# Two unused 32-byte tiles that shift every tile of on-chip memory by 32 bytes

## The chip, the cores and the metric

The kernel runs on one core of one Trainium2 chip. TensorE (PE) multiplies matrices, VectorE (DVE), ScalarE (ACT) and GpSimd (POOL) work element by element, SyncE (SP) issues nearly all transfers. All share the on-chip memory: 128 partitions, and a tile takes the same byte range of each. Products go to eight banks of accumulation memory. A matmul has two operands in on-chip memory: the stationary one, which a weight load (PEld) brings into the array, and the moving one, which streams through, one column at a time. The metric is the device time of one execution in microseconds, as a median of several runs.

## The reference

```python
mod = (_silu(c) @ w_mod).reshape(c.shape[0], 6, 1, -1)
sa, ca, ga, sb, cb, gb = (mod[:, 0], mod[:, 1], mod[:, 2], mod[:, 3], mod[:, 4], mod[:, 5])
h = _layernorm(x, axis=-1) * (1 + ca) + sa
x = x + ga * _A_ref(h, A_wqkv, A_wo)
h = _layernorm(x, axis=-1) * (1 + cb) + sb
x = x + gb * _B_ref(h, B_w1, B_b1, B_w2)
```

x is 2048 rows of 448 numbers in float32. `_A_ref` is attention with 16 heads of width 28 over a sliding window of 256 rows; `_B_ref` is a dense layer from 448 to 1792, mish (x tanh(softplus(x))), and a dense layer back to 448. The modulation vectors come from c, one row.

## The kernel before

The rows are worked in four groups of 512 (g = 0 to 3). To hold float32 accuracy, each operand of a large product is split into a high part, in TensorE's rounded float32 format, and a low part, the rest; a product is then three passes per 128 of the inner size (high by high, high by low, low by high), eleven matmuls over 448 inner rows.

Three stages follow each other. In the first 40 us the first rows of x, the modulation weights and the projection weights are loaded and split, and the first q and k tiles are made (L490). From there to about 440 us attention runs, head by head: `A` makes scores for the row maxima (sA, L675, read by DVE with the mask at L677), `M2` turns the maxima and sends them into the q tile by a transfer, `B` makes the shifted scores (sB, L705, and masks through L716), ACT takes the exponential twice (L719, L720), POOL makes the low part (L727), `PV` multiplies by v (pv, L737), `E` turns the result (L751), and POOL scales it into the tile `on` (L767). Between these steps a list of fillers issues the projections of the next group (qk and qk_v, L311), the output projection (wo, L311) and the normalisations, at a rate written out by hand. From about 440 us the dense layers run in 56 steps, 14 for each group: eleven matmuls for z (L912, moving operand the normalised rows `hh` and `hl`, weights from `w13` and `w1l`), mish on ACT (L918), a split (L919, L920), and twelve matmuls for the output of the step before (acc, L1095 to L1097, moving operand `w2h` or `w2l`, weights `ah` or `al`). The program text gives the order of the instructions on every engine; the allocator doesn't change it.

On-chip memory is a pair of stacks of pools. The left stack grows upward, in this order: `cst` (constants, among them `cT`, `ident`, `ones`, `cols`), `mid` (hh, hl, output weights, `on`), `vp` (six of the ten v tiles), `kq` (k tiles, mask, first q tile), `st0` (staging for the first loads), which `att` (other q tiles, P, Ph, Pl) replaces at L510, and later `ff` in the place of vp, kq and att (L1084). The right stack grows downward from the end: `vq` (four v tiles), `qk` (x tiles, `wq3`, `wql`), and later `w1p` in the place of both (L824; it holds w13, w1l, ah, al, t) and `tmp` (L826). A tile takes a multiple of 32 bytes. By the allocator's listing of this kernel the tiles start as follows, in bytes of a partition:

| tile | stack | start | beyond a multiple of 64 |
|---|---|---|---|
| cT, ones, cols | left | 16512, 17088, 17600 | 0 |
| ident | left | 16544 | 32 |
| hh (and all of mid) | left | 19680 | 32 |
| v0 / k3_0 / P | left | 62944 / 85984 / 126752 | 32 |
| xin / wq3 / wql | right | 147488 / 155680 / 177184 | 32 |
| w13 / w1l / ah | right | 148832 / 177504 / 219104 | 32 |
| v6 | right | 213984 | 32 |

The right stack ends at 229344; the left one reaches 147232 at its highest, while the right one begins at 147488. The large tiles are all 32 beyond; rows inside them step by multiples of 64 bytes, except the heads of v (240 bytes each) and of `on` (112 bytes each).

Of the kernel before, what the change touches and what calls it, by code (L numbers as in the profile page):

```python
# [8 lines left out]
F32 = mybir.dt.float32  # L9
# [42 lines left out]
def adaln_block(ctx: ExitStack, tc: tile.TileContext, x, wqkv, wo, w1, b1, w2, c, w_mod, out):  # L52
# [8 lines left out]
    def pool(name, side="left", space=None):  # L61
        kw = {} if space is None else {"space": space}
        cm = tc.tile_pool(name=name, bufs=1, reuse_waits="tile", side=side, **kw)
        st = ExitStack()
        return st.enter_context(cm), st
# [4 lines left out]
    cst, cst_s = pool("cst")  # L70
    mid, mid_s = pool("mid")
    vp, vp_s = pool("vp")
    kq, kq_s = pool("kq")
    st0, st0_s = pool("st0")
    vq, vq_s = pool("vq", side="right")
    qk, qk_s = pool("qk", side="right")
    ctx.enter_context(tc.manual_schedule())

    cT = cst.tile([112, 4], F32, name="cT")
    nc.scalar.dma_start(cT, c.rearrange("o (k p) -> p (o k)", p=112))  # L80
    ACT.add_instruction(mybir.InstLoadActFuncSet(
# [697 lines left out]
    FW = {}  # L779
# [177 lines left out]
    def fill_side(g):  # L957
        if g + 1 < NG:
            yield from ln1[g + 1]
            while g + 1 not in ht_done:  # L960
                yield
            yield from lazy((gen_mod_wo, lambda: gen_mod_ln2(3), lambda: gen_mod_ln2(4))[g])
            if g == NG - 2:
                yield from gen_out_load()
            return
        yield from gen_out_sum()
        while g not in w1_ready:
            yield
        yield from gen_w1()
# [12 lines left out]
    side = {g: fill_side(g) for g in range(NG)}  # L982
# [43 lines left out]
    for u in range(NU + 9):  # L1026
        s, k = divmod(u, 3)
# [56 lines left out]
    ff, ff_s = pool("ff")  # L1084
# [41 lines left out]
    def fill_step():  # L1126
        if fill is not None:
            pipe.step()
            next(fill, None)
            flush()  # L1130
    for n in range(NN + 1):
# [14 lines left out]
        if n:  # L1146
# [2 lines left out]
            ff2(n - 1)  # L1149
            for _ in range(1 + (g == 0) + (n == 1)):  # L1150
                fill_step()
    for st in (ff_s, mid_s, cst_s, FW["s"], psf_s):
        st.close()


# [21 lines left out]
```

## Time and profile before

| what | us |
|---|---|
| median of three runs | 720.67 |
| the runs | 719.48, 723.41, 720.67 |
| span of the profiled execution | 719.3 |

The page of the profile gives busy time by engine, the chain of work that ended last (followed backward from the last instruction, at each step to what released it), and groups of instructions by line. Matmuls are pipelined: one starts before the one before it ends, so their busy times overlap, and what one costs is the distance of its start from the next start. The chain view shows that: its pieces follow each other without overlap. The rows themselves stand in the prediction.

### The profile page before, as it was taken

What the parts mean: (1) busy time and instruction counts of PE and PEld (TensorE: products, weight loads), DVE (VectorE), ACT (ScalarE), POOL (GpSimd) and SP (SyncE); (2) the same over time, 40 slices, a digit from 0 to 9 for tenths busy, and PEclk for the clock granted to TensorE, in tenths of its full rate; (3) what the DMA queues carried; (4) which work ended last, traced back from release to release, by engine and by line L of the source; (5) the groups of instructions that cost most, each with busy time, mean ns of one, the idle gap of its engine ahead of it and who ended that gap; (6) DMA issues with size and microseconds to landing.
All of it is one profiled execution on the core that took longest, in us unless ns stands there. A gap on an engine that the chain in (4) does not pass through costs nothing.

```text
span 719.3 us, 12057 instructions
## 1 busy us (share of the span) xinstructions
PE 694.8 (97%) x4049; PEld 595.9 (83%) x4049; DVE 380.0 (53%) x1018; ACT 390.8 (54%) x740; POOL 326.5 (45%) x358
## 2 busy tenths in 40 slices
PE   8899999999999999999999899999999999999996
PEld 8777778788898788898887688888888888888885
DVE  5588657688555878555768642334223222322112
ACT  4538778767666758666878864243224222422221
POOL 6536679576765767666879754332010000000002
PEclk9999999999999999999999999999999999999999
DMA  7865854454771562744782175300200020001001
GB/s 213 258 211 178 249 185 138 136 160 139 200 217 50 178 190 75 220 158 127 227 225 75 52 237 143 108 1 14 90 1 1 13 90 1 1 13 39 0 1 51
DMA packets 48249, 83.86 MB, mean 117 GB/s; under 512 B 6142, under 2 KB 26348, under 8 KB 48188
## 3 DMA queue, kind: packets, MB, share of 16 engines
q1 hardware_dynamic: 47724, 83.10, 38.0%
q8 instruction: 32, 0.52, 0.3%
q14 instruction: 29, 0.24, 0.1%
q10 hardware_dynamic: 464, 0.00, 0.0%
HBM read 53.45 MB, written 29.36 MB: 115 GB/s over the span
## 4 chain that ended last, share of the span: by engine, by line
PE 72%; issue 11%; DVE 8%; DMA 4%; ACT 2%; POOL 1%; SPq 1%; POOLq 0%; DVEq 0%; ACTq 0%
PE z L912 15%; PE pv L737 9%; PE qk L311 8%; PE sA L675 5%; PE acc L1096 5%; PE acc L1097 5%; PE acc L1095 5%; PE sB L705 4%; PE wo L311 4%; PE qk_v L311 4%; PE sB L716 3%; DVE junk L677 3%; PE et L751 2%; DMA q<-mr 1%; PE warm L424 1%
## 5 line engine op out<-in xcount | busy, mean ns | idle before, releaser
L727 POOL TENSOR_TENSOR Pl<-P,Ph 128x512 fp32r<-128x512 f32 (+2 forms) x192 | 234.3, 1228 | 87.1 <-ACT Ph L720 48.4
L677 DVE CUSTOM_DVE_ANT_0 junk<-sA,mask 128x384 f32<-128x384 f32 (+2 forms) x256 | 135.1, 528 | 98.7 <-PE sA L675 90.1
L719 ACT ACTIVATE P<-sB 128x512 f32<-128x512 f32 (+2 forms) x192 | 109.7, 571 | 66.7 <-PE sB L716 61.0
L920 DVE TENSOR_TENSOR al<-t,ah 128x512 fp32r<-128x512 f32 x56 | 38.7, 692 | 200.0 <-ACT ah L919 200.0
L918 ACT ACTIVATE t<-z,b1c 128x512 f32<-128x512 f32 x56 | 38.5, 687 | 189.3 <-PE z L912 178.4
L720 ACT ACTIVATE Ph<-sB 128x512 fp32r<-128x512 f32 (+2 forms) x192 | 109.4, 570 | 0.0
L675 PE MATMUL sA<-k,q 84*128 84x384 f32 (+2 forms) x256 | 101.0, 396 | 2.5 <-DVE mx L677 1.5
L912 PE MATMUL z<-hhf,w 128*128 128x512 f32 x224 | 89.6, 400 | 0.0
L912 PE MATMUL z<-hlf,w 128*128 128x512 f32 x224 | 88.8, 396 | 0.0
L1095 PE MATMUL acc<-w2h,ah 128*128 128x448 f32 x224 | 82.1, 367 | 0.0
L1096 PE MATMUL acc<-w2l,ah 128*128 128x448 f32 x224 | 82.1, 367 | 0.0
L1097 PE MATMUL acc<-w2h,al 128*128 128x448 f32 x224 | 82.0, 366 | 0.0
L737 PE MATMUL pv<-Ph,v 128*60 128x256 f32 (+2 forms) x352 | 77.1, 293 | 3.5 <-DVE o L745 2.3
L737 PE MATMUL pv<-Pl,v 128*60 128x256 f32 (+2 forms) x352 | 74.2, 285 | 2.3 <-POOL Pl L727 2.3
L705 PE MATMUL sB<-q,k 86*128 86x256 f32 (+1 forms) x352 | 74.5, 285 | 1.7 <-DMA q<-mr 1.7
L912 PE MATMUL z<-hhf,w1l 128*128 128x512 f32 x168 | 66.4, 395 | 0.0
L705 PEld LDWEIGHTS sB<-q,k 86*128 86x128 f32 x352 | 62.3, 191 | 3.2 <-DMA q<-mr 1.4
L737 PEld LDWEIGHTS pv<-Ph,v 128*60 128x60 f32 x352 | 45.7, 134 | 18.2 <-ACT o L743 3.2
L716 PE MATMUL sB<-fdmask,identr 128*128 128x128 bf16 (+1 forms) x320 | 60.4, 254 | 0.0
L675 PEld LDWEIGHTS sA<-k,q 84*128 84x128 f32 x256 | 48.9, 192 | 8.9 <-DVE mx L677 5.9
L737 PEld LDWEIGHTS pv<-Pl,v 128*60 128x60 f32 x352 | 45.4, 132 | 10.9 <-POOL Pl L727 3.9
L1104 POOL TENSOR_TENSOR yo<-yo,x 128x448 f32<-128x448 f32 (+1 forms) x4 | 4.1, 1057 | 108.6 <-DVE yo L1101 108.6
(156 smaller groups left out, 1297.4 us busy)
## 6 DMA issues: line engine op xcount, KB each, us to landing
scr<-st SPq DMA_DIRECT2D x24, 512.0 KB
k<-scr SPq DMA_DIRECT2D x48, 252.0 KB
q<-scr SPq DMA_DIRECT2D x64, 168.0 KB
scr<-st SPq DMA_DIRECT2D x32, 256.0 KB
x<-x1d SPq DMA_DIRECT2D x10, 448.0 KB
xin<-in_A_x_dram SPq DMA_DIRECT2D x8, 448.0 KB
xr<-in_A_x_dram SPq DMA_DIRECT2D x16, 224.0 KB
x1d<-xr SPq DMA_DIRECT2D x16, 224.0 KB
```

The source lines that it names most:

```text
L311: PE.matmul(p, b, a, start=(n == 0), stop=(n == 10))
L675: PE.matmul(p[:, c0:384], q[0:84, t * 128:(t + 1) * 128], k[0:84, t * 128 + c0:t * 128 + 384], start=True, stop=True)
L677: DVE.tensor_tensor_reduce(out=junk[:, c0:384], in0=p[:, c0:384], in1=mask[:, c0:384], scale=1.0, scalar=-3.0e38, op0=ALU.add, op1=ALU.max ...
L705: PE.matmul(p[:, c:c + 128 * (t1 - t0)], k[:, jj * 128:(jj + 1) * 128], q[:, t0 * 128:t1 * 128], start=(n == 0), stop=False, skip_group_ch ...
L719: ACT.activation(P[:, c0:], p[:, c0:], AF.Exp, scale=SCALE)
L720: ACT.activation(Ph[u][:, c0:], p[:, c0:], AF.Exp, scale=SCALE)
L727: eng.tensor_tensor(Pl[u][:, a:b], Pt[u][:, a:b], Ph[u][:, a:b].bitcast(F32), op=ALU.subtract)
L737: PE.matmul(pv[0:60, t0 * 128:t1 * 128], V[j % NV][:, h, :], P[u][:, c:c + 128 * (t1 - t0)], start=(P is Ph and b == 0 and n == 0), stop=F ...
L912: PE.matmul(zb[n], ps[m][1], ps[m][0], start=(m == 0), stop=(m == 10))
L1095: PE.matmul(p, ah[n][:, ts], w2h[f], start=(f == 0), stop=False)
L1096: PE.matmul(p, ah[n][:, ts], w2l[f], start=False, stop=False)
L1097: PE.matmul(p, al[n][:, ts], w2h[f], start=False, stop=(f == NF - 1))
```

## The change

One tile of 32 bytes (`lead`) is allocated as the first of the left stack's first pool, and a pool `edge` with one tile of 32 bytes is opened as the first of the right stack. Nothing writes or reads them. The pool is closed at the end of the program in its turn.

```diff
@@ -72,10 +72,13 @@
     vp, vp_s = pool("vp")
     kq, kq_s = pool("kq")
     st0, st0_s = pool("st0")
+    edge, edge_s = pool("edge", side="right")
+    edge.tile([128, 8], F32, name="edge")
     vq, vq_s = pool("vq", side="right")
     qk, qk_s = pool("qk", side="right")
     ctx.enter_context(tc.manual_schedule())
 
+    cst.tile([128, 8], F32, name="lead")
     cT = cst.tile([112, 4], F32, name="cT")
     nc.scalar.dma_start(cT, c.rearrange("o (k p) -> p (o k)", p=112))
@@ -1149,7 +1152,7 @@
-    for st in (ff_s, mid_s, cst_s, FW["s"], psf_s):
+    for st in (ff_s, mid_s, cst_s, FW["s"], edge_s, psf_s):
         st.close()
```

All other tiles of the left stack move up by 32 bytes, those of the right stack down by 32: hh to 19712, k3_0 to 86016, wq3 to 155648, w13 to 148800, all multiples of 64, while cT, ones and cols come to lie 32 beyond.

## The prediction

> **What bounds the kernel now.** I read the page first (engine shares, then the chain), then the busy times by stage, then the chain inside each stage.
>
> ```profile
> span 719.3 us, 12057 instructions
> PE 694.8 (97%) x4049; PEld 595.9 (83%) x4049; DVE 380.0 (53%) x1018; ACT 390.8 (54%) x740; POOL 326.5 (45%) x358
> ...
> PE 72%; issue 11%; DVE 8%; DMA 4%; ACT 2%; POOL 1%; SPq 1%; POOLq 0%; DVEq 0%; ACTq 0%
> ```
>
> ```profile
> 0.00:40.00 40.00, 35.90 (x205) 31.43 (x206) 24.88 (x58) 18.36 (x32) 22.80 (x57) 1.00 0.80 236
> 40.00:440.00 400.00, 386.29 (x2570) 329.03 (x2569) 272.72 (x832) 289.98 (x580) 275.91 (x265) 1.00 0.54 164
> 440.00:720.00 280.00, 272.60 (x1277) 235.48 (x1276) 82.35 (x129) 82.42 (x129) 27.77 (x36) 0.99 0.10 31
> ```
>
> The columns after the stretch's length are busy time and instructions of PE, PE's weight loads, DVE, ACT and POOL, then the granted clock, the DMA share and GB/s. TensorE is busy nearly without a break at full clock; DMA fills the first 40 us only. So a change of addresses is worth what it does to TensorE's operand reads, and the other engines matter by their shares of the chain alone.
>
> ```profile
> by line: PE pv L737 15.9%; PE qk L311 14.1%; PE sA L675 8.8%; PE sB L705 7.9%; PE qk_v L311 6.4%; PE wo L311 5.8%; PE sB L716 5.4%; DVE junk L677 4.9%; PE z L912 3.2%; issue 3.1%; PE et L751 2.7%; DMA q<-mr 2.5%; DVE tr L250 1.7%; DVE hl L2
> ```
>
> This is the chain from 40 to 440 us. Its PE entries sum to 70%, 281 of 400 us. From 440 us on PE alone sets the pace. So of the matmuls about 0.70 x 2570 + 1277 = 3080 stand on the path, and 1 ns on each of them is 3.1 us.
>
> What one of them takes is read from starts on the chain, since the busy times of pipelined matmuls overlap:
>
> ```profile
> 490.53 0.44 PE trf L246 x4
> ...
> 495.95 2.57 PE z L912 x11
> ...
> 500.94 2.57 PE z L912 x11
> ...
> 511.02 2.57 PE z L912 x11
> 516.07 2.57 PE z L912 x11
> ```
>
> ```profile
> 253.19 0.47 PE pv L737 x4
> 253.66 0.24 PE sB L705 x2
> ```
>
> Eleven matmuls of 512 columns take 2.57 us, 0.2336 us each. The twelve of 448 columns between 498.52 (495.95 + 2.57) and 500.94 take 2.42 us, 0.2017 us each. In attention four pv matmuls, 1024 columns, take 0.47 us, 0.235 us per 512; two sB matmuls, 512 columns, take 0.24 us.
>
> **The change part by part.** Two tiles that nothing writes or reads are allocated, and one pool is opened and closed: no instruction, no DMA, no semaphore, no bytes moved. What changes is addresses. By the allocator's listing of the kernel before, every tile of the left stack goes up by 32 bytes and every tile of the right stack down by 32; both stacks keep their inner order, so which tile lies where another lay stays the same, and no wait for reuse is added. Between the stacks 256 bytes are free at their tightest, 192 after; no tile of one lies over one of the other. Removed and added instructions: 0 us.
>
> So every term is a rate: does an operand that starts on a multiple of 64 cost other than one that starts 32 beyond? The trace of before has controls, since some operands already start elsewhere.
>
> ```profile
> L737 PEld LDWEIGHTS pv<-Ph,v x352: 129/133/239, 50.9 to 416.9; 128*60 128x60 f32 x176
> ...
> L737 PEld LDWEIGHTS pv<-Pl,v x352: 129/131/217, 51.2 to 417.1; 128*60 128x60 f32 x176
> ```
>
> ```profile
> L912 PEld LDWEIGHTS z<-hhf,w x224: 187/188/197, 413.7 to 706.9; 128*128 128x128 f32 x112
> ```
>
> ```profile
> L552 PEld LDWEIGHTS ga<-wm,ones x2: 186/188/189, 91.1 to 91.2; 112*128 112x128 f32 x2
> ```
>
> Weight loads (three numbers: least, median, most, in ns). Head h of v starts at 32 + 240h bytes, so the heads run through 32, 16, 0 and 48 beyond a multiple of 64, a quarter each. If a quarter were quicker, the least would stand well below the median; it stands 2 to 4 ns below. The tile ones lies on a multiple of 64 now and loads in a median of 188 ns, as w13 does from 32 beyond. I price weight loads at 0, bounds -2 to +2 ns, and they overlap the running matmul anyway.
>
> ```profile
> L767 POOL TENSOR_TENSOR on<-ol,rc x32: 554/563/572, 68.2 to 422.6; 128x224 f32<-128x224 f32 x32
> ```
>
> ```profile
> 0.72 0.20 POOL masks.py:197 MEMSET ident<- 128x128 f32 x1 [0.29 <-POOLq L1165]
> ...
> 1.24 0.20 POOL L141 MEMSET ones<- 112x128 f32 x1
> ```
>
> Writes by POOL: heads in pairs advance 224 bytes in the tile on, so half of these 32 writes begin on a multiple of 64 and half 32 beyond: 554 to 572 ns, one cluster. The memsets of ident (32 beyond) and ones (a multiple) both take 0.20 us. Price 0.
>
> ```profile
> L677 DVE CUSTOM_DVE_ANT_0 junk<-sA,mask 128x384 f32<-128x384 f32 x224 | 123.9, 553 | 81.9 <-PE sA L675 77.4
> ...
> L677 DVE CUSTOM_DVE_ANT_0 junk<-sA,mask 128x256 f32<-128x256 f32 x16 | 6.7, 417 | 3.2 <-PE sA L675 2.8
> ```
>
> DVE takes (553 - 417) / 128 = 1.06 ns per element. Its 8% of the chain is 58 us, about 105 instructions of 553 ns; at most one piece of 64 bytes (16 elements, 17 ns) saved in each is -1.8 us, the other end 0. ACT's 2% is a quarter of that. DMA's 4% is 29 us; a piece of 2048 bytes over 32 instead of 33 units of 64 is at most 3%, -0.9 us. I take 0 for all three, by the POOL rows, which are nearest.
>
> The moving operand of a matmul is what no row shows: all of them start 32 beyond now. Bound from the rows: a cost at the start must show where 512 columns are cut in two. The pv pairs cost 0.235 - 0.2336 = 1.4 ns more than one matmul, the sB pairs 0.24 - 0.2336 = 6.4 ns. A start thus costs 1.4 to 6.4 ns in all, whatever its reason, and alignment can win at most this: -4 to -20 us over 3080 matmuls. The other end is a loss of the same size as two rhythms seen in the trace, priced below. Between ends that far apart I take 0, by the weight loads, the nearest reads by the same engine. The Trainium skill (SBUF — State Buffer, Specifications) gives the memory's lines as 16 bytes; 32 beyond is already on such a line, so by that rule the sum is exactly 0, while the trace agrees for weight loads only (131 and 133 ns at offsets 0 to 48).
>
> Sum: 719.3 us span + 0 = 719.3. The runs have a median of 720.67, 1.4 us above the profiled span (their least, 719.48, is 0.2 above it); with that 1.4 the forecast is 720.
>
> **The rivals.**
>
> *A start on a full line of 64 saves part of each start.* For it: a cost of 6.4 ns per start of sB is there, and z at 512 columns is slower than twice the transposes' pace would give. Against it: the pv pairs show 1.4 ns, and weight loads show nothing. Middle of 4 and 20 us: 720.7 - 12 = 709, from 701 to 716.
>
> *The whole stream is slowed by straddling.* If each 64 bytes of the stream are fetched across two lines, the cost runs with the columns. Four transposes of 128 columns take 0.44 us; if a plain pass can go at twice that pace, an estimate from this row, 512 columns take 0.22 us. Then z gains 13.6 ns x 11 and acc 9.2 ns x 12 per step, 260 ns, 14.6 us over 56 steps; in attention 0.2375 becomes 0.22, 7.4% of 281 us = 20.8 us. Result 685. Against it: the excess may be how these passes run. The Trainium skill (TensorE: Matmul & The Clock Gate, Back-to-back issue gap) gives N/2.4 + 2.5 ns, 216 ns for 512 and 189 ns for 448 columns; by it the same sum wins about 42 us, 679. The trace stands above that page by 17 ns.
>
> *Slower: the distance between the two stacks.* Left goes up and right goes down, so a matmul whose moving operand lies left and whose weights lie right sees them 64 bytes closer. That address relations may matter is seen in the step: 495.95 to 500.94 is 4.99 us, 511.02 to 516.07 is 5.05 us with the same 2.57 us in z, so twelve acc matmuls cost 2.48 instead of 2.42 us, 5 ns each, with other w2 tiles as moving operand. If the new distance puts all such matmuls into the slow rhythm: z and acc 1277, qk and qk_v (20.5% of 400 us at 0.234 us) 350, together 1627; half of acc, 336, I count as slow already, leaving 1290 x 5 ns = 6.5 us: 727. It decides from 3.6 / 1.29 = 2.8 ns per matmul. Against it: pv reads its moving operand from the left stack and v from either stack (six of its ten tiles left, four right), and the loads of v keep one median over both; no row ties the step's two rhythms to distance.
>
> *The change does not do what it says.* If an unused tile got no room, addresses stay and the time is 720.7; this falls in with the forecast.
>
> **How the numbers follow.** What differs by less than 0.5%, 3.6 us, can't be told from no change in runs that spread from 719.5 to 723.4. Chances: no effect 0.37, part of each start 0.29, the whole stream 0.12, slower rhythm 0.22. A cheap end of the second (under 3.6 us) is too small a part to move. So faster 0.41, same 0.37, slower 0.22, and the likeliest single case is 720. Cases of both signs hold most of the chance: the forecast's own range is 717 to 724. The range from 700 to 731 holds no effect, the partial gain and the slower rhythm up to 8 ns per matmul (10.3 us), and leaves out the whole-stream case and the slower tail, some 0.17.
>
> **What would show it.** Right: z still 2.57 us for eleven, acc 2.42 or 2.48 us for twelve, pv 0.47 us for four, weight loads 188 and 131 ns, and the same number of instructions in the same order. A gain at starts: z, pv and sB shorter by the same few ns whatever their columns, so sB pairs gain twice what z gains. The whole stream: the gain goes with the columns, z near 2.42 us for eleven. The slower rhythm: every step at 5.05 us or more, wo (both operands left) unchanged while z, acc and qk lengthen. The forecast is wrong if PE's starts move at all beyond 1 ns each; it is wrong in another place if PE's starts stay and DMA landings or DVE's idle time before L677 move.

## The result and the profile after

The changed kernel takes 718.18 us as a median of nine runs (716.06 to 719.96), the kernel before 720.67 in nine runs beside it (719.09 to 723.41). The ratio is 0.9966 with a 95% interval from 0.9949 to 0.9982: a gain of 2.5 us, small but not nothing. The profiled execution is the slowest of the nine, 719.96 us with a span of 718.2, where the other eight have spans from 714.3 to 717.3. So the two profiled spans, 719.3 and 718.2, understate the gain, and stages are compared below, not spans.

The page of the kernel after, busy times, the main queue and the chain by engine:

```profile
span 718.2 us, 12057 instructions
...
PE 694.9 (97%) x4049; PEld 597.3 (83%) x4049; DVE 380.0 (53%) x1018; ACT 390.9 (54%) x740; POOL 327.0 (46%) x358
...
q1 hardware_dynamic: 47724, 83.10, 37.1%
...
PE 72%; issue 11%; DVE 8%; DMA 4%; ACT 2%; POOL 1%; SPq 1%; POOLq 0%; DVEq 0%; ACTq 0%
```

The counts are the same on every engine, and their order in the two traces is too. The stretches by stage, same columns as before:

```profile
0.00:40.00 40.00, 36.74 (x206) 32.26 (x206) 25.16 (x59) 18.34 (x32) 23.04 (x57) 0.96 0.78 236
40.00:440.00 400.00, 386.69 (x2568) 329.59 (x2567) 272.52 (x831) 289.81 (x580) 276.09 (x265) 0.99 0.53 164
440.00:720.00 280.00, 271.51 (x1279) 235.44 (x1277) 82.37 (x129) 82.79 (x129) 27.83 (x36) 0.99 0.10 31
```

The granted clock reads 0.96 and 0.99 in the first two stretches where the kernel before had 1.00 twice; that belongs to this execution, the slowest of the nine. In the dense stage both have 0.99, and there the traces can be compared. The chain of the kernel after, at the places that the prediction quoted:

```profile
495.92 2.56 PE z L915 x11
...
500.91 2.56 PE z L915 x11
...
510.88 2.57 PE z L915 x11
...
515.86 2.56 PE z L915 x11
```

The step that took 4.99 us still does (500.91 - 495.92). The step that took 5.05 us now takes 4.98 (515.86 - 510.88), with the same 2.57 us in z: the gain sits in the twelve acc matmuls of the steps that were slow. Over all 56 steps, the mean from one start to the next in the trace:

```
ns from start to start           before    after
acc, 448 columns, f = 0 to 6      205.9    201.1
acc, 448 columns, f = 7 to 13     202.9    203.4
z, 512 columns                    233.0    232.8
first acc to last acc, us         291.76   290.22
```

In this table f is the place of a step among the 14 of its group. 28 steps x 12 x (-4.8 ns) + 28 x 12 x 0.5 + 56 x 11 x (-0.2) = -1.6 us, against 291.76 - 290.22 = 1.54 us measured. Of the other operations, qk went from 233.1 to 231.3 ns, qk_v from 202.1 to 203.6, wo from 205.1 to 204.2. A second trace of the kernel before, told of below, has 233.1, 202.3 and 204.2: there qk and qk_v stay where they were, while the fall of wo is no more than two traces of one kernel differ by. The controls, from the instructions by line and tile of the kernel after:

```profile
L740 PEld LDWEIGHTS pv<-Ph,v x352: 129/133/240, 50.7 to 417.4; 128*60 128x60 f32 x176
```

```profile
L915 PEld LDWEIGHTS z<-hhf,w x224: 187/188/264, 414.1 to 705.8; 128*128 128x128 f32 x112
```

```profile
L770 POOL TENSOR_TENSOR on<-ol,rc x32: 557/564/571, 67.8 to 423.2; 128x224 f32<-128x224 f32 x32
```

```profile
L680 DVE CUSTOM_DVE_ANT_0 junk<-sA,mask 128x384 f32<-128x384 f32 x224 | 123.9, 553 | 82.6 <-PE sA L678 78.1
```

Weight loads, POOL and DVE kept their times within 1 ns (medians of 133, 188 and 564 ns, and a mean of 553 for DVE). What is left is the pace at which the moving operand streams: it changed by a few ns, in some passes and not in others.

### The profile page after: what moved, and what is told of

It is laid out like the page before. It is cut to its first block, busy times and chain, and to the rows that moved or that the text cites. A ratio compares the mean times of both kernels' runs of the same rounds, so it can differ in the third digit from the quotient of the medians.

```text
span 718.2 us, 12057 instructions
## 1 busy us (share of the span) xinstructions
PE 694.9 (97%) x4049; PEld 597.3 (83%) x4049; DVE 380.0 (53%) x1018; ACT 390.9 (54%) x740; POOL 327.0 (46%) x358
## 3 DMA queue, kind: packets, MB, share of 16 engines
q1 hardware_dynamic: 47724, 83.10, 37.1%
## 4 chain that ended last, share of the span: by engine, by line
PE 72%; issue 11%; DVE 8%; DMA 4%; ACT 2%; POOL 1%; SPq 1%; POOLq 0%; DVEq 0%; ACTq 0%
PE z L915 15%; PE pv L740 9%; PE qk L314 8%; PE sA L678 5%; PE acc L1098 5%; PE acc L1100 5%; PE acc L1099 5%; PE sB L708 5%; PE wo L314 4%; PE qk_v L314 4%; PE sB L719 3%; DVE junk L680 3%; PE et L754 2%; DMA q<-mr 1%; DMA scr<-st 1%
## 5 line engine op out<-in xcount | busy, mean ns | idle before, releaser
L740 PE MATMUL pv<-Pl,v 128*60 128x256 f32 (+2 forms) x352 | 74.4, 286 | 2.3 <-POOL Pl L730 2.3
```

The source lines that it names most:

```text
L740: PE.matmul(pv[0:60, t0 * 128:t1 * 128], V[j % NV][:, h, :], P[u][:, c:c + 128 * (t1 - t0)], start=(P is Ph and b == 0 and n == 0), stop=F ...
```

## The experiments

Two theories. **Place** (A): what counts is whether an operand starts on a multiple of 64; the expectations of the first runs take this for the transfers above all. **Distance** (B): what counts is how far the moving operand lies from the weights (its address less theirs), modulo some power of two; the change moves the left stack by +32 and the right one by -32, so for a matmul with its moving operand left and its weights right the distance grows by 64. The expectations name a third, C: any displacement changes the time by chance.

**One side at a time.** The first run keeps only the tile `lead`, the second only the tile `edge`. Each aligns one of the two stacks and changes the distance by 32.

```diff
+    cst.tile([128, 8], F32, name="lead")
```

```diff
+    edge, edge_s = pool("edge", side="right")
+    edge.tile([128, 8], F32, name="edge")
...
-    for st in (ff_s, mid_s, cst_s, FW["s"], psf_s):
+    for st in (ff_s, mid_s, cst_s, FW["s"], edge_s, psf_s):
```

> Only the left stack moves (up 32 bytes, to multiples of 64); the right one stays 32 beyond. Theory A, transfers that read or write on-chip memory are dearer from 32 beyond: the packets of 1792 bytes that leave the left stack (x1d and out) take 74 ns instead of 76 to 79 ns, those of st (right stack) stay; ratio about 0.998. Theory B, the matmuls' rhythm follows the distance between the stacks: twelve acc matmuls leave 2.42 or 2.48 us by over 0.02 us, and the ratio may fall on either side of 1. Theory C, any displacement does it by chance: ratio anywhere in 0.994 to 1.006.

> Only the right stack moves (down 32 bytes). Theory A: packets from the left stack stay at 76 to 79 ns, those stored from st get shorter; ratio about 0.998, and the two halves together give the whole change (0.9966). Theory B: the distance of the stacks changes by the same 32 bytes as with the left alone, so acc and z come out as with the left alone. Theory C: no relation to the halves.

Measured: 720.05 us, ratio 1.0001 [0.9988, 1.0014], and 719.98 us, 1.0001 [0.9985, 1.0016]. The chain of the first:

```profile
576.87 2.57 PE z L913 x11
...
581.91 2.58 PE z L913 x11
...
586.96 2.58 PE z L913 x11
```

Steps of 5.04 and 5.05 us, as before. Neither alignment alone gives a half of the gain, or any that can be measured. Theory B came true in part: the two sides come out alike, as it said, but it had also expected the twelve acc matmuls to leave their 2.42 and 2.48 us by over 0.02 us, and they stay within that (a mean of 204.4 and 204.5 ns for one, 204.4 before).

**Both sides by 64 and by 96.** Both tiles as `[128, 16]`, then as `[128, 24]` (the diff of the change with this number). With 64 every large tile stays 32 beyond a multiple of 64; with 96 every one is aligned, as in the change. The distance grows by 128 and 192.

> Both tiles are 64 bytes: every tile moves by 64, so all large ones stay 32 beyond a multiple of 64. Theory A: nothing gained, ratio 1.000 within 0.0015, packets of x1d and out at 76 to 79 ns. Theory B: the distance changes by 128 bytes, twice that of the change, so the acc times change too. Theory C: a ratio other than 1 is as likely as with the change.

> Both tiles are 96 bytes: every large tile lies on a multiple of 64 again, at other places than with the change (64 beyond a multiple of 256 on the left instead of 0). Theory A with 64 bytes as the unit: ratio 0.9966 within 0.0015 as with the change, packets at 74 ns. If 256 bytes are the unit, packets stay at 76 to 79 ns and the ratio at 1.000. Theory B: the distance changes by 192 bytes, acc times other than with the change. Theory C: no relation.

Measured: 718.33 us, 0.9977 [0.9963, 0.9991], and 717.87 us, 0.9965 [0.9952, 0.9977]. The first gains without any alignment. The second has the ratio that Theory A had expected, so taken alone it would fit both theories. The chain of the first shows where the gain lies:

```profile
581.56 2.53 PE z L915 x11
...
586.54 2.53 PE z L915 x11
```

Here z takes 2.53 us for eleven and acc 4.98 - 2.53 = 2.45, 0.04 and 0.03 us less than in the steps of 5.05 us. Over all steps acc keeps its mean of 204.4 ns (1.9 ns less where f is 0 to 6, 1.9 more where it is 7 to 13), and z falls from 233.0 to 230.0: on balance the gain is in another operation than in the change.

**The pace by itself.** A kernel of matmul blocks alone, 40 each, on two tiles whose bases are a multiple of 256 bytes apart; weights step by 512 bytes. The block's first letter is its width (L 512, K 448, S 128 columns), the second the start of the moving operand (a, b, c, d, e at 0, 16, 32, 48, 96 bytes), the third that of the weights (a, c at 0 and 32); `dist` blocks move the moving operand by 0, 64, 128, 256 to 2048 bytes. Behind them stand element-wise passes and transfers at several offsets. The kernel before ran once more with it.

```python
for i in range(40):
    PE.matmul(p[i % 2][:, 0:cols], W[:, w + 128 * (i % 4):w + 128 * (i % 4) + 128], X[:, m:m + cols], start=True, stop=True)
```

> Computes nothing of the reference: loads, matmuls, element-wise instructions and stores of one shape each, with operands at 0, 16, 32, 48 and 96 bytes beyond a multiple of 256 (transfers at more places). Prediction's own step: matmul starts, weight loads, ACT, DVE and POOL equal within 1 ns at all places. Rival, a start on a line of 64 saves: 1 to 6 ns less per matmul at 0 than at 32, the same for 128 and 512 columns. Rival, the stream straddles: about 14 ns less at 0 for 512 columns, 3 to 4 ns for 128. Theory A: stores of 1792 bytes 2 to 5 ns a packet shorter from 0 and 64 than from 32 and 96; loads equal.

> The kernel before, unchanged, for the spread of a profile: PE starts and packet times of late stores (76 to 79 ns) come back as in the first profile, and the DMA queue's share within 0.3 of 38.0%. If the late stores come out at 74 ns here, Theory A falls.

The kernel before again took 718.94 us in a single run, with 204.0 and 233.0 ns for acc and z (first trace 204.4 and 233.0) and a dense stage of 291.31 us (291.76): between two traces of one kernel the dense stage moves by about 0.5 us. The chain of the blocks (start, us for 40):

```profile
53.78 9.07 PE mmLaa L74 x40
62.86 9.33 PE mmLac L74 x40
72.19 9.27 PE mmLba L74 x40
81.46 9.46 PE mmLbc L74 x40
90.92 9.33 PE mmLca L74 x40
100.25 9.07 PE mmLcc L74 x40
...
118.65 9.27 PE mmLdc L74 x40
```

For 512 columns this settles it. Both operands at 0 (aa) and both at 32 (cc) take the same 9.07 us; one of them at 32 (ac, ca) takes 9.33. A moving operand 16 bytes further than the weights takes 9.27 with the weights at 0 (ba) and at 32 (dc). The distance sets the pace, the place does not. The prediction's own step, which this run's expectation gave as equal within 1 ns, fails here: the blocks of 512 columns spread over 9.07 to 9.46 us, 226.8 to 236.5 ns each. The passes of 128 columns took 4.42 to 4.47 us for 40 at every distance. Element-wise passes don't mind either, from the view of the tile Z, each group over four combinations of offsets 0 and 32:

```profile
L89 ACT ACTIVATE Z<-Y x16: 629/629/630, 331.4 to 341.3; 128x512 fp32r<-128x512 f32 x16
...
L94 DVE TENSOR_TENSOR Z<-Y x16: 691/692/694, 342.4 to 353.3; 128x512 fp32r<-128x512 f32 x16
...
L98 POOL TENSOR_TENSOR Z<-Z,Y x16: 1262/1262/1262, 354.1 to 374.2; 128x512 fp32r<-128x512 f32 x16
```

**The same distance without alignment, and a whole period.** First `lead` alone as `[128, 16]`: the distance of the change (+64), every large tile 32 beyond. Then both tiles as `[128, 32]`: +256. Beside them the map of the pace, blocks as above with the moving operand 0 to 512 bytes further, and a version with distances chosen from the blocks above, told of below.

> Only the left stack moves, by 64 bytes: all large tiles stay 32 beyond a multiple of 64, but moving operand and weights come 64 bytes closer, as with the change. Theory B (the distance between the two operands within 256 bytes sets the pace): start to start, acc 202.3 and z 232.8 ns as with the change, dense stage 290.2 us instead of 291.8, ratio 0.9965 to 0.9985. Theory A (alignment to 64): acc 204.4, z 233.0 ns, ratio 1.000 within 0.0015.

> Both tiles are 128 bytes, distance changed by 256. Theory B with a period of 256 bytes: acc 204.4 and z 233.0 ns as before, dense stage 291.8 us, ratio 1.000 within 0.0015. If the period is longer, they differ. Theory C (any displacement): a ratio of 0.997 is as likely as in the other displacements.

> Computes nothing of the reference: matmuls of 512 and of 448 columns with the weights fixed and the moving operand 0, 32, 64 and so on up to 256, 288, 320 and 512 bytes further. Theory B: 226.7 ns at 0 and about 229 at 64 for 512 columns, 231 to 234 at 32, 96 and 128; 206.7 at 0 and 200.0 at 64 for 448 columns; 288 and 320 like 32 and 64. Theory A: equal at 0, 64, 128, 192 and another value at 32, 96, 160, 224.

With +64 by one side alone: 718.71 us, 0.9978 [0.9967, 0.9988], acc 202.3 and z 232.8 ns, which are the means of the change (202.3, 232.8), and a dense stage of 290.21 us (290.22). Its chain has steps of 4.96 and 4.99 us where the kernel before has 5.05:

```profile
576.28 2.56 PE z L913 x11
581.24 2.57 PE z L913 x11
586.23 2.56 PE z L913 x11
```

With +256: 720.31 us, 1.0006 [0.9992, 1.002], acc 204.4, z 233.0 and 291.76 us, which are those of the kernel before, and steps of 5.05 us:

```profile
578.89 2.57 PE z L915 x11
583.94 2.57 PE z L915 x11
```

So the period divides 256 bytes, and all of the dense stage's gain is distance. Theory C falls too: two pairs of kernels at other addresses but equal distances have the same dense stage within 0.01 us. The map (start, us for 40; a, b, c, d, e, f, g, h are 0 to 224 bytes in steps of 32, i 256, k 320):

```profile
53.86 9.07 PE mLa L74 x40
62.93 9.34 PE mLb L74 x40
72.27 9.16 PE mLc L74 x40
...
90.76 9.33 PE mLe L74 x40
...
109.46 9.33 PE mLg L74 x40
...
128.12 9.09 PE mLi L74 x40
...
146.55 9.16 PE mLk L74 x40
...
164.80 8.11 PE mKa L74 x40
...
181.17 8.00 PE mKc L74 x40
...
197.38 8.15 PE mKe L74 x40
...
230.06 8.27 PE mKi L74 x40
...
246.50 8.00 PE mKk L74 x40
```

For 512 columns distance 0 is the quickest (226.8 ns each), 64 next (229.0), the rest near 233. For 448 columns 64 is the quickest (200.0). At distance 0 and 256 they have two rhythms, 8.11 and 8.27 us (202.8 and 206.8 ns), though 206.7 was expected at 0. The first kernel of blocks differs in the same way between distances that are whole periods apart, 8.31 us at 0 (distp) and 8.11 at 512 (distt):

```profile
272.65 8.31 PE distp L74 x40
...
305.22 8.11 PE distt L74 x40
```

So for 448 columns the distance is not all that counts; nor is 288 quite like 32 there (8.18 and 8.27 us).

**Chosen distances.** The blocks ask for distance 0 in z and 64 in acc. In the kernel before z is at 128 and acc at 0, but for the `w2l` of f = 7 to 13, which lie 64 further. `edge` of 64 bytes brings acc to 64, a gap of 64 behind `w1l` brings z to 0, and a gap of 192 ahead of the tiles of f = 7 brings them into line. The first version leaves the left stack where it was, all large tiles 32 beyond; the second is the change with the two gaps, all aligned; the third is the first again, beside the second.

```diff
+    edge.tile([128, 16], F32, name="edge")
...
         w1l = FW["w1l"] = p1.tile([128, 3, F], F32R, name="w1l")
+        p1.tile([128, 16], F32, name="gap")
...
         pl = FW["p1"] if f == 0 else FW["ff"]
+        if f == 7:
+            pl.tile([128, 48], F32, name="gap7")
```

> Distances chosen apart for the two products: the right stack 64 bytes down, 64 unused bytes between w1l and ah, 192 in ff ahead of w2l7, so that hh and hl start at the same place within 256 bytes as w13 and w1l (0, where the rates run has 226.7 ns for 512 columns), w2h and w2l 64 beyond ah and al (200.0 ns for 448), and qk at 0. All large tiles stay 32 beyond a multiple of 64. Theory B: z 227 to 230 ns, acc 200 to 202 ns, dense stage 284 to 288 us, ratio 0.988 to 0.995. Theory A: 1.000 within 0.0015.

> The change as it is (32 bytes at each end, large tiles on multiples of 64) plus the two gaps of the run with chosen distances: the same distances (0 for z, 64 for acc, 0 for qk), but aligned. Theory B alone: z 227.8, acc 200.3 ns, dense stage 285.9 us as without alignment, and the same ratio, 0.992 within 0.0015. If alignment adds something of its own (Theory A in the transfers of the first 440 us), up to 1 us less, ratio 0.9905.

> The run with chosen distances and all large tiles 32 beyond a multiple of 64, once more on the same chip as its aligned twin, for a direct comparison: ratio 0.992 within 0.0015, z 227.8 and acc 200.3 ns.

Measured: 714.55 us, 0.9922 [0.9905, 0.9939]; 714.30 us, 0.9919 [0.9903, 0.9935]; 714.64 us, 0.9925 [0.9908, 0.9941]. All three beat both kernels. The stretch and the chain of the first:

```profile
440.00:720.00 280.00, 264.34 (x1265) 232.67 (x1263) 80.30 (x125) 80.94 (x125) 26.00 (x35) 0.99 0.10 31
```

```profile
577.56 2.49 PE z L917 x11
...
582.46 2.49 PE z L917 x11
...
587.35 2.49 PE z L917 x11
```

Steps of 4.90 and 4.89 us (acc 2.41 and 2.40), at the same granted clock of 0.99. The second, aligned, has the same 2.49 us in z and a step of 4.89:

```profile
580.31 2.49 PE z L918 x11
...
585.20 2.49 PE z L918 x11
```

With the distances equal, alignment is worth nothing that these runs can tell. All runs together, from the traces and the timings:

```
                 distance   large tiles  acc    z      dense   ratio
                 z    acc   beyond 64    ns     ns     us
before           128  0     32           204.4  233.0  291.76  1
left 32          160  32    0 / 32       204.4  233.6  291.99  1.0001
right 32         160  32    32 / 0       204.5  233.6  292.11  1.0001
the change       192  64    0            202.3  232.8  290.22  0.9966
left 64          192  64    32           202.3  232.8  290.21  0.9978
both 64          0    128   32           204.4  230.0  289.89  0.9977
both 96          64   192   0            202.9  230.8  289.38  0.9965
both 128         128  0     32           204.4  233.0  291.76  1.0006
chosen           0    64    32           200.3  227.8  285.85  0.9922
chosen, aligned  0    64    0            200.3  227.6  285.83  0.9919
```

In every row the `w2l` of f = 7 to 13 lie 64 further than the column says, but for the last two; and the w2 tiles of f = 0, which lie in the right stack with ah, are at 0 throughout. Some things the map does not give: at distance 0, z is 230.0 ns with acc at 128 and 227.8 with acc at 64 (226.8 alone), and at 64 it is 230.8 (229.0 alone). In attention qk (hh against wq3, by the listing of the tiles) went from 192 to 0 with the change and gained 1.8 ns, where the map has 6.5; qk_v, whose weights lie left and whose moving operand lies right, went from 64 to 0 and lost 1.5, where the map has 2.8 or 6.8. The signs are the map's, the sizes are not. A pass seems to depend on the pass beside it too; that was not tried by itself.

## Why the prediction was right, and where not

**The time.** 718.18 lies in both ranges that the prediction gives and 1.8 us under its forecast of 720; the ratio's interval lies within 0.5% for all but its lower end (0.9949). So the forecast of no effect within 0.5% came near, but of the zeros in its sum one was wrong. That the zero cost so little was luck: the change happens to move z between two distances of equal pace and helps one half of the acc steps only. Other shifts by unused bytes, the chosen distances, took 5.9 us off the dense stage alone, and 714.55 us lies outside 717 to 724.

**Right.** No instruction, transfer or semaphore was added, and no order changed. Weight loads, POOL, DVE and ACT cost nothing, as their rows said. z stayed at 2.57 us for eleven, and pv and sB at their durations, from the chain after:

```profile
251.56 0.47 PE pv L740 x4
252.03 0.24 PE sB L708 x2
```

The Trainium skill (SBUF — State Buffer, Specifications) gives lines of 16 bytes, from which the prediction took that 32 beyond is as good as a multiple of 64; for the place of an operand the runs agree, since 0 and 32 gave the same 9.07 us.

**The step that failed.** The prediction priced the moving operand at 0 "by the weight loads, the nearest reads by the same engine", and called itself wrong if PE's starts moved "at all beyond 1 ns each". They did: acc by 2.1 ns in the mean, by 4.8 ns where f is 0 to 6, and qk by 1.8 ns. A weight load read alone can't show this, because the price belongs to the pair, as ac and ca against aa and cc show: where the moving operand lies relative to the weights. That the stream and the weight loads beside it are what meets is argued, not shown. Nor did the bounds for the moving operand rest on much: its 6.4 ns for a start came from a row of 0.24 us, and the last digit of that row is worth 10 ns.

**The rivals.** Those of a full line and of straddling fell: aligning one side gives 1.0001 twice, the shift by 64 gains at 32 beyond, and the aligned and unaligned versions with equal distances have 0.9919 and 0.9925. The rival of the distance between the two stacks named the true mechanism, in the right place (the acc matmuls of the steps at 5.05 us) and of the right size (it said 5 ns each), but with the wrong sign: it took the kernel before to be partly in the slow rhythm and the change to put all of it there. In fact the acc of f = 0 to 6 stood in it and the new distance, 64, is the quickest for 448 columns. z went from 128 to 192, which the map holds to be equal (9.33 us both). Its +6.5 us became -1.5. Its sum also counted qk_v with the moving operand left, where it lies right. The second price of straddling comes to about 45 us by its own terms (19.4 in the dense layers and 25.4 in attention), not 42.

**The transfers.** The share of the main queue fell from

```profile
q1 hardware_dynamic: 47724, 83.10, 38.0%
```

on the page before to 37.1%. Alignment doesn't explain it: `both 96` and `chosen, aligned` have 38.0% and 37.9%. In the traces the stores of 1792 bytes after 640 us have a median of 74 ns a packet, 76 before. With `lead` alone they have 74 too, at a ratio of 1.0001, so this is not where the time came from. They have 73 in `both 64` and `left 64`, from 32 beyond, so Theory A has the wrong rule for them as well.

**Left open.** The dense stage accounts for 1.5 us of the 2.5 us between the medians. The rest falls ahead of it, or in the spread. The changed pace of qk and qk_v is worth some tenths of a us by the trace's means: about 240 qk in the chain (14.1% of 400 us at 233.1 ns) gain 1.8 ns each, 0.4 us, and about 130 qk_v lose 1.5 each, 0.2 us. The spread is larger than what is missing: from the first pv to the first acc the traces of this document take 366.8 to 367.7 us where the granted clock reads 1.00 throughout, and 369.8 and 370.1 where it reads 0.991 in the mean. `left 64`, with the same distances, gains 1.6 us between its medians (720.35 and 718.71), which is what the dense stage says.

## What to carry to other kernels

Where a kernel is bound by a dense run of matmuls, measure their start-to-start time at several distances between moving operand and weights within 256 bytes, by themselves and at the widths in use, and set the distances by gaps between tiles; here gaps of 64 to 192 bytes gave 0.8% of the whole. Only one format and weights of 128 x 128 were tried. A change that shifts addresses should be read as a change of all distances between operands, and tested with a shift that keeps the place and changes the distance, and the other way round. A row of one operand alone can't bound a cost that belongs to two.

## What the runs showed of the hardware

The pace of a matmul in the rounded float32 format, with its weight load beside it, depends on the distance from weights to moving operand, and for 512 columns the values at 256 and 320 bytes are those at 0 and 64 within 0.02 us for 40. For 512 columns it runs from 226.8 ns to 236.5 ns (9.46 us for 40, weights at 32 and the moving operand at 16). The Trainium skill (TensorE: Matmul & The Clock Gate, Step-by-step: what each phase is for) says that PE has two independent read ports, one for the stream and one for weight loads: "Loading the next tile's weights doesn't steal SBUF read bandwidth from the running matmul." By that the distance should not matter, and these runs disagree by up to 9.7 ns of 236.5. No run here streams without weight loads, so what the loads cost in all isn't shown. Why the period is 256 bytes (no half of it, since 512 columns take 9.07 us at 0 and 9.33 at 128), and what picks one of the two rhythms at distance 0 for 448 columns, stays open.

Stores take a little longer when their source starts late in a stretch of 256 bytes, as far as tried: those of the output after 640 us, 1792 bytes a packet, have a mean of 73.7 ns at 0 (the change), 73.5 at 32 (`both 64`), 74.4 at 64 (`both 96`), 75.4 at 96 (`both 128`) and 77.2 at 224 (the kernel before), the starts by the allocator's listing. Loads of 1792 bytes have a median of 74 ns at every offset from 0 to 224 in the first kernel of blocks.
